# Queries in three parts with one load per lane, products over 48 and 50 rows, query sums by fours

## The chip, the cores and the metric

The kernel runs on one core of a Trainium2 chip. The metric is the device time of one execution, in microseconds; for a kernel the median of its runs stands.

## What is computed

One transformer block with conditioning: two layer norms modulated by a vector c, attention of 32 heads that share one key and value head of 16 columns, and a dense part of 512 to 1376 to 512 with gelu. All is float32, S = 2048 rows, D = 512.

```python
mod = silu(c) @ w_mod                      # sa, ca, ga, sb, cb, gb
h = layernorm(x) * (1 + ca) + sa
q = (h @ wq) as 32 heads of 16;  k = h @ wk;  v = h @ wv      # one k, one v
o = softmax(q @ k.T * 16 ** -0.5) @ v
x = x + ga * (o @ wo)
h = layernorm(x) * (1 + cb) + sb
x = x + gb * (gelu(h @ w1 + b1) @ w2 + b2)
```

## The kernel before

**Tiling.** The rows are cut into 8 blocks of 256 (HQ); each block has 8 units of 4 heads, so there are 64 units. A unit goes over the 2048 keys in 8 half-steps; the main loop (from L1424) takes two of them, X and Y, per iteration. The array of TensorE is used as two lanes of 64 rows by 128 columns: lane s = 0 uses array rows 0 to 63, lane s = 1 rows 64 to 127, each for two heads, and the lanes run side by side.

**Queries.** A projection's result is split into a high and a low part (qH, qL, float32r), which `send_q` (L436) stores in the DRAM tile dq. `load_q` (L487) brings a unit's queries back as the tile qst, one of four buffers: in each lane, rows 0 to 47 hold high, low and high part of 16 columns of q, rows 48 and 49 the high and low part of minus the row's maximum, rows 50 to 63 zeros. The key tile ks has -1 in rows 48 and 49. So one product of qst and ks gives scores less their maxima.

**Two passes.** `Max.step` (L516) makes the products m (L526) of a later unit, with rows 48 and 49 still zero; VectorE reduces each at L531. When half of a unit's maxima are done, the queries of the next unit are loaded (L534); when all are done, `put_max` (L550) turns them, splits them on POOL (L587, L141, L148) and `send` (L563) writes them by DMA into rows 48 and 49. `sexp` (L625) makes the products e (L649) from the finished qst; ScalarE takes their exponentials p (L657). The products acc (L674) multiply p with the values. A half-step has four m, four e, sixteen acc and in most of the program up to six side products, which all lie on one lane.

**Side products.** `half` (L207) issues one half of a side product on a lane. Sums of them (query projections qps, wops, w1ps, w2ps) are cut into batches, one for each iteration: lane 0 makes its half of the batch in one half-step, lane 1 its half in the next. A late query projection is `qproj_late` (L469): 12 products, so 24 halves, in batches of BATCH = 6 where (block, group) lies under LONG, else SHORT = 4. Long sums are copied out by VectorE (L477), short ones by ScalarE (L475).

**Order.** The five engines' instructions are issued in the order in which this code is run. `clock[0]` counts ticks, four per iteration; `later(n, fn)` puts work off by n ticks. At the end of an iteration (L1568) one turn of the weights' preparation is made (`state["turns"]` is 1 there): for w2 a piece is loaded, multiplied by gb on POOL (L1237) and split there (L141, L148) into w2H, w2L. There are 11 pieces. POOL also works for gelu: `inner` (L1017), a square on ScalarE (L1018) and two operations on POOL (L1019, L1020); then `tanh` on ScalarE (L1023), and the rest on POOL (L1029, L1030). The sync queue (SP) issues all DMAs.

Of the kernel before, what the change touches and what calls it, by code (L numbers as in the profile page):

```python
# [8 lines left out]
F32 = mybir.dt.float32  # L9
# [5 lines left out]
P = 128  # L15
# [21 lines left out]
MAX_WAIT = (1, 4)  # L37
QBUFS = 4
PREP = 4
BUSY = 5  # L40
BATCH = 6
SHORT = 4
LONG = (3, 1)
TAIL = (14, 9, 7)
EARLY = 5
HELD = 4
# [11 lines left out]
def raw(ap):  # L58
    return ap.bitcast(F32)
# [3 lines left out]
def adaln_mqa_mlp(  # L63
# [15 lines left out]
    nc = tc.nc  # L79
    _, S, D = x.shape  # L80
# [11 lines left out]
    HQ = BQ // 2  # L92
# [31 lines left out]
    gb = const.tile([P, D], F32, name="gb")  # L124
    b2g = const.tile([P, D], F32, name="b2g")

    dq = [[tc.dram_tile([2, 4, 16, 2, BQ], F32, name=f"dq_{b}_{g}") for g in range(KD)] for b in range(NB)]
    dz = tc.dram_tile([2, 2, HQ], F32, name="dz")
    dw1 = tc.dram_tile([NF, P, 2, KD, P], F32, name="dw1")
    drs = [tc.dram_tile([H, w], F32, name=f"drs{b}") for b, (_, w) in enumerate(blocks)]  # L130
    do = [tc.dram_tile([H // 4, 4, 32, w], F32, name=f"do{b}") for b, (_, w) in enumerate(blocks)]
# [1 line left out]
    turns = [0]  # L133
# [17 lines left out]
    clock = [0]  # L151
    state = {"mods": False, "q": NB * KD, "busy": False, "turns": 1, "lanes": (1, 0)}
# [103 lines left out]
    qbufs = [att.tile([P, 2, HQ], F32R, name=f"qst{i}") for i in range(QBUFS)]  # L256
# [1 line left out]
    qbufs = [att.tile([P, 2, HQ], F32R, name=f"qst{i}") for i in range(QBUFS)]  # L258

    def load_constants():  # L260
        nc.sync.dma_start(out=dz, in_=raw(qbufs[0][48:50]))
        with nc.allow_non_contiguous_dma(reason="1376 numbers"):
            nf_full = F // P
            nc.sync.dma_start(out=b1c[:, :nf_full], in_=b1[0:nf_full * P].rearrange("(f p) -> p f", p=P))
            if F % P:
                nc.gpsimd.memset(b1c[:, nf_full:NF], 0.0)
                nc.sync.dma_start(out=b1c[:F % P, nf_full:NF], in_=b1[nf_full * P:F].rearrange("(p f) -> p f", f=1))
# [44 lines left out]
    nc.gpsimd.memset(raw(wkL), 0.0)  # L312
    nc.gpsimd.memset(raw(ks), -1.0)
    nc.gpsimd.memset(va[:, :, 16:32], 1.0)
    for qst in qbufs:
        nc.gpsimd.memset(raw(qst), 0.0)

    def prep_wkv():
        for o, n, src in ((0, 3, 0), (48, 1, Dh), (64, 3, 0)):
# [114 lines left out]
        nc.scalar.copy(va[:, b * QT:(b + 1) * QT, 0:Dh], pv_[:, :, 16:32])  # L434

    def send_q(b, g, qH, qL):  # L436
        for t, src in enumerate((qH, qL)):
            nc.sync.dma_start(out=dq[b][g][t].rearrange("a r j n -> (a r j) n"), in_=raw(src))
        state["q"] -= 1
        sent.add((b, g))  # L440

    sent = set()
# [44 lines left out]
    def load_q(u):  # L487

        b, Q = units[u]
        r0, w = blocks[b]  # L490
        qst = qsts[u] = qbufs[u % QBUFS]
        h, g, a0 = r0 // BQ, Q // 2, (Q % 2) * 2
        cols = slice(r0 % BQ, r0 % BQ + w)
        assert (h, g) in sent
        for s in range(2):
            for r, part in ((0, 0), (16, 1), (32, 0)):
                nc.sync.dma_start(out=raw(qst[64 * s + r:64 * s + r + 16]), in_=dq[h][g][part, a0 + s][:, :, cols])
            if u >= QBUFS:
                nc.sync.dma_start(out=raw(qst[64 * s + 48:64 * s + 50]), in_=dz)

    class Max:

# [16 lines left out]
        def step(self, s, hold=None, **place):  # L519
            u, j, t, kc = self.todo[s].pop(0)  # L520
            T = blocks[units[u][0]][1] // P
            if u not in self.mx:
                self.mx[u] = att.tile([P, 4 * T, NKC], F32, name=f"mx{u}", tag="mx", bufs=2)
            m = psum.tile([P, 512], F32, name=f"m{u}_{j}_{t}_{kc}_{s}", **(place or dict(tag="m", bufs=3)))
            rows = slice(64 * s, 64 * s + 64)
            nc.tensor.matmul(m, qsts[u][rows, j, t * P:(t + 1) * P], ks[rows, kc * 512:(kc + 1) * 512],  # L526
                             start=True, stop=True)
            i = (s * 2 + j) * T + t

            def reduce():  # L530
                nc.vector.tensor_reduce(out=self.mx[u][:, i, kc:kc + 1], in_=m, axis=AX.X, op=ALU.max)  # L531
                self.left[u] -= 1
                if self.left[u] == size[u] // 2 and u > 1 and u + 1 < NU:
                    load_q(u + 1)  # L534
                if self.left[u] == 0:
                    put_max(u, self.mx.pop(u))

            self.done += 1
            if hold is None:
                reduce()  # L540
            else:
                hold(reduce)
# [7 lines left out]
    def put_max(u, mx):  # L550

        T = blocks[units[u][0]][1] // P
        qst = qsts[u]
        mm = mms[u % 2]
        turned = att.tile([P, 32], F32, name=f"turned{u}", tag="turned", bufs=2)
        if u == 0:
            pad(att, 256, "pad7")
        mt = att.tile([4 * T, P], F32, name=f"mt{u}", tag="mt", bufs=2)  # L560
        mh = att.tile([4 * T, P], F32R, name=f"mh{u}", tag="mh", bufs=2)
        ml = att.tile([4 * T, P], F32R, name=f"ml{u}", tag="ml", bufs=2)

        def send():
            for s in range(2):
                for r, src in ((48, mh), (49, ml)):
                    dst = qst[64 * s + r:64 * s + r + 1].rearrange("p j (t n) -> p (j t) n", n=P)
                    nc.sync.dma_start(out=raw(dst), in_=raw(src[2 * T * s:2 * T * (s + 1), :].unsqueeze(1)))
            placed.add(u)

        def place_first():
            for i in range(2):
                for g, piece in ((32 * i, lambda d, s: nc.scalar.copy(d, s)),
                                 (64 + 32 * i, lambda d, s: nc.gpsimd.tensor_scalar(out=d, in0=s, scalar1=1.0, scalar2=0.0, op0=ALU.mult, op1=ALU.add))):
                    piece(mt[:, g:g + 32], turned[g:g + 4 * T, :])

            def send_row(r, src):
                dst = qst[r:r + 65:64].rearrange("p j (t n) -> p (j t) n", n=P)
                nc.sync.dma_start(out=raw(dst), in_=raw(src.unsqueeze(1)))

            split(mh, ml, mt, nc.scalar, nc.gpsimd, lambda: send_row(48, mh))
            send_row(49, ml)
            placed.add(u)

        def gather():
            for g in range(0, P, 32):
                nc.gpsimd.tensor_scalar(out=mt[:, g:g + 32], in0=turned[g:g + 4 * T, :], scalar1=1.0, scalar2=0.0,  # L587
                                        op0=ALU.mult, op1=ALU.add)
            split(mh, ml, mt, nc.gpsimd, nc.gpsimd)

        def reduce():
            nc.vector.tensor_reduce(out=mm[:, :4 * T], in_=mx, axis=AX.X, op=ALU.max)
            nc.vector.transpose(out=turned, in_=mm)  # L593
            if u == 0:
                place_first()
                return
# [31 lines left out]
    def sexp(u, K, j, s, line=None):  # L628

        w = blocks[units[u][0]][1]  # L630
        qst = qsts[u]
        assert u in placed
        n = u * steps[0] + K
        if n < 3 and n not in pbufs:
            pbufs[n] = att.tile([P, 2, 2, 512], F32, name=f"p{n}", tag="p", bufs=3)
        pt = pbufs[n % 3]
        bank = banks.pop(0)
        if not bare[0]:
            banks.append(bank)
        if not isinstance(bank, int):  # L640
            e = bank
        else:
            e = psum.tile([P, 512], F32, name=f"e{u}_{K}_{j}_{s}", tag=f"e{bank}", bufs=1)
        rows = slice(64 * s, 64 * s + 64)
        if w == 512:
            kt, rhs = K, qst[rows, j, :]
        else:
            kt, rhs = 2 * K + j, qst[rows].rearrange("p j n -> p (j n)")
        nc.tensor.matmul(e, ks[rows, kt * P:(kt + 1) * P], rhs, start=True, stop=True)  # L649
        dst = pt[:, j, s, :]  # L650

        state["last"] = e

        def exp():
            if bare[0]:
                banks.append(bank)
            ins = nc.scalar.activation(dst, e, AF.Exp, scale=0.25)  # L657
            for old in written.pop((n - 3, j, s), ()):
                tc.declare_no_dep(ins.ins, old, reason="the products that read the tile's last contents come between the two")
            written.setdefault((n, j, s), []).append(ins.ins.name)  # L660
            return ins

        return exp() if line is None else line.append(exp)
# [756 lines left out]
    for u in range(NU):  # L1420
        for K in range(0, steps[u], 2):
# [145 lines left out]
                preps["w2"] = prep_w2()  # L1567
            if clock[0] >= prepared[0] + PREP and weights and weights[0] in preps and not state["busy"]:  # L1568
                prepared[0] = clock[0]
                for _ in range(state["turns"]):  # L1570
                    if weights and next(preps[weights[0]], 0) == 0:
                        weights.pop(0)
    end_step(*behind)
# [55 lines left out]
```

## Time and profile before

| | |
|---|---|
| median of 3 runs | 1549.43 us (1548.95 to 1549.63) |
| the profiled execution | 1549.17 us |
| its span, first to last instruction | 1547.4 us |
| granted TensorE clock | 1.000 over the span |
| busy: TensorE, VectorE, ScalarE, POOL | 1531.7, 1397.7, 1227.9, 666.6 us |

The profile is of one execution. Busy time is what an engine spends in instructions that compute; PE is TensorE, PEld its loading of weights, DVE VectorE, ACT ScalarE, and SPq the sync engine's queue, whose instructions issue DMAs. The chain that ended last is followed backwards from the end: each step goes to what released it, or to the instruction ahead of it on its engine. In tables of windows, an engine's busy time in a stretch stands beside the stretch's length. In timelines an "xN" is a run of like instructions, and square brackets hold the idle time ahead of an instruction with what ended it by the profile.

### The profile page before, as it was taken

What the parts mean: (1) busy time and instruction counts of PE and PEld (TensorE: products, weight loads), DVE (VectorE), ACT (ScalarE), POOL (GpSimd) and SP (SyncE); (2) the same over time, 40 slices, a digit from 0 to 9 for tenths busy, and PEclk for the clock granted to TensorE, in tenths of its full rate; (3) what the DMA queues carried; (4) which work ended last, traced back from release to release, by engine and by line L of the source; (5) the groups of instructions that cost most, each with busy time, mean ns of one, the idle gap of its engine ahead of it and who ended that gap; (6) DMA issues with size and microseconds to landing.
All of it is one profiled execution on the core that took longest, in us unless ns stands there. A gap on an engine that the chain in (4) does not pass through costs nothing.

```text
span 1547.4 us, 41604 instructions
## 1 busy us (share of the span) xinstructions
PE 1531.7 (99%) x16421; PEld 956.1 (62%) x16421; DVE 1397.7 (90%) x2493; ACT 1227.9 (79%) x2400; POOL 666.6 (43%) x1224
## 2 busy tenths in 40 slices
PE   7999999999999999999999999999999999999999
PEld 4555555567655665557655676556655676557668
DVE  7999999999999999999999999999999999999914
ACT  5677778788778887788877887788877888778874
POOL 6445524866322570246521462235711474046511
PEclk9999999999999999999999999999999999999999
DMA  8246312312030211203112120302212230213141
GB/s 261 83 132 190 133 46 91 122 59 89 16 111 19 84 60 36 94 28 101 30 51 81 55 88 23 104 26 95 62 30 74 61 100 25 84 31 99 49 151 49
DMA packets 84203, 120.85 MB, mean 78 GB/s; under 512 B 21330, under 2 KB 57426, under 8 KB 83752
## 3 DMA queue, kind: packets, MB, share of 16 engines
q1 hardware_dynamic: 84008, 118.19, 23.5%
q8 instruction: 130, 2.13, 0.6%
q14 instruction: 65, 0.53, 0.1%
HBM read 90.87 MB, written 26.74 MB: 76 GB/s over the span
## 4 chain that ended last, share of the span: by engine, by line
PE 89%; DVE 9%; DMA 1%; ACT 0%; issue 0%; POOL 0%; SPq 0%; DVEq 0%; ACTq 0%
PE acc L674 31%; PE m L526 24%; PE e L649 16%; DVE mx L531 8%; PE w1ps L207 8%; PE w2ps L207 3%; PE w2ps L196 1%; PE qps L207 1%; PE w1ps L196 1%; PE wops L207 1%; PE tp L207 1%; DVE st L859 0%; DMA wm<-in_w_mod_dram 0%; DVE x L852 0%; PE wops L196 0%; PE modr L291 0%
## 5 line engine op out<-in xcount | busy, mean ns | idle before, releaser
L531 DVE TENSOR_REDUCE mx<-m 128x1 f32<-128x512 f32 x2048 | 1269.3, 681 | 82.9 <-PE m L526 61.5
L657 ACT ACTIVATE p<-e 128x512 f32<-128x512 f32 x2048 | 1098.3, 598 | 254.7 <-PE e L649 109.3
L526 PE MATMUL m<-ks,qst 64*128 64x512 f32 x2048 | 835.2, 429 | 2.2 <-ACT bigH L394 0.8
L649 PE MATMUL e<-qst,ks 64*128 64x512 f32 x2048 | 744.3, 411 | 0.2 <-DMA qst<-ml 0.2
L674 PE MATMUL acc<-p,va 128*32 128x256 f32 x8192 | 546.9, 385 | 0.0
L526 PEld LDWEIGHTS m<-ks,qst 64*128 64x128 f32 x2048 | 366.8, 184 | 202.5 <-DVE mx L531 172.2
L649 PEld LDWEIGHTS e<-qst,ks 64*128 64x128 f32 x2048 | 364.1, 184 | 83.9 <-ACT p L657 61.7
L674 PEld LDWEIGHTS acc<-p,va 128*32 128x32 f32 x8192 | 214.9, 109 | 213.2 <-issue 109.1
L207 PE MATMUL w1ps<-h2H,w1t 64*128 64x256 f32 x1232 | 235.4, 287 | 0.0
L587 POOL TENSOR_SCALAR mt<-turned 8x32 f32<-8x32 f32 x252 | 52.3, 208 | 402.8 <-DVE turned L593 390.9
L207 PEld LDWEIGHTS w1ps<-h2H,w1t 64*128 64x128 f32 x1232 | 185.8, 184 | 28.8 <-DVE mx L531 16.0
L207 PE MATMUL w1ps<-h2L,w1t 64*128 64x256 f32 x616 | 169.2, 275 | 0.0
L207 PE MATMUL w2ps<-w2H,gH 64*128 64x512 f32 x288 | 127.2, 442 | 0.3
L207 PEld LDWEIGHTS w1ps<-h2L,w1t 64*128 64x128 f32 x616 | 114.2, 185 | 0.0
L207 PE MATMUL w2ps<-w2L,gH 64*128 64x512 f32 x288 | 112.9, 392 | 0.0
L207 PE MATMUL w2ps<-w2H,gL 64*128 64x512 f32 x288 | 112.3, 390 | 0.0
L1019 POOL TENSOR_SCALAR tt<-tt 128x256 f32<-128x256 f32 x77 | 31.0, 403 | 132.2 <-ACT tt L1018 97.3
L207 PEld LDWEIGHTS w2ps<-w2H,gH 64*128 64x128 f32 x288 | 52.9, 184 | 12.8 <-issue 2.9
L148 POOL TENSOR_TENSOR gL<-z,gH 128x256 fp32r<-128x256 f32 x77 | 56.8, 738 | 6.4
L1020 POOL TENSOR_TENSOR tt<-tt,z 128x256 f32<-128x256 f32 x77 | 56.7, 737 | 6.4
L1030 POOL TENSOR_TENSOR z<-tt,z 128x256 f32<-128x256 f32 x77 | 56.3, 731 | 6.0
L1029 POOL TENSOR_TENSOR tt<-tt,z 128x256 f32<-128x256 f32 x77 | 56.4, 732 | 0.0
(199 smaller groups left out, 1474.4 us busy)
## 6 DMA issues: line engine op xcount, KB each, us to landing
w1t<-dw SPq DMA_DIRECT2D x82, 512.0 KB
qst<-dq SPq DMA_DIRECT2D x384, 32.0 KB
do<-oc SPq DMA_DIRECT2D x62, 128.0 KB
dw<-w1s SPq DMA_DIRECT2D x11, 512.0 KB
xt<-in_A_x_dram SPq DMA_DIRECT2D x4, 1024.0 KB
dq<-qH SPq DMA_DIRECT2D x16, 256.0 KB
dq<-qL SPq DMA_DIRECT2D x16, 256.0 KB
x<-in_A_x_dram SPq DMA_DIRECT2D x8, 512.0 KB
```

The lines of the kernel that those rows point to most:

```text
L148: eng_l.tensor_tensor(out=dst_l, in0=src, in1=raw(dst_h), op=ALU.subtract)
L207: ins = nc.tensor.matmul(ps, a[rows], b_[rows], start=first_ and turn == 0, stop=last_ and turn == 1)
L526: nc.tensor.matmul(m, qsts[u][rows, j, t * P:(t + 1) * P], ks[rows, kc * 512:(kc + 1) * 512], start=True, stop=True)
L531: nc.vector.tensor_reduce(out=self.mx[u][:, i, kc:kc + 1], in_=m, axis=AX.X, op=ALU.max)
L587: nc.gpsimd.tensor_scalar(out=mt[:, g:g + 32], in0=turned[g:g + 4 * T, :], scalar1=1.0, scalar2=0.0, op0=ALU.mult, op1=ALU.add)
L649: nc.tensor.matmul(e, ks[rows, kt * P:(kt + 1) * P], rhs, start=True, stop=True)
L657: ins = nc.scalar.activation(dst, e, AF.Exp, scale=0.25)
L674: ins = nc.tensor.matmul(accs[u][32 * cidx:32 * cidx + 32, :], va[:, kt, :], rhs, start=kt == 0, stop=kt == NKT - 1)
L1019: nc.gpsimd.tensor_scalar(out=tt, in0=tt, scalar1=1.0, scalar2=1.0, op0=ALU.mult, op1=ALU.add)
L1020: nc.gpsimd.tensor_tensor(out=tt, in0=tt, in1=z, op=ALU.mult)
L1029: nc.gpsimd.tensor_tensor(out=tt, in0=tt, in1=z, op=ALU.mult)
L1030: nc.gpsimd.tensor_tensor(out=z, in0=tt, in1=z, op=ALU.add)
```

## The change

1. dq holds three parts, high, low, high, in two halves of 256 rows. `send_q` stores with three DMAs instead of two, and `load_q` loads a lane with one DMA of 48 rows instead of three of 16 (and none of zeros). The tile of zeros dz, its DMA and the four clearings of the buffers go.
2. `send` writes a row of maxima of both lanes with one DMA, so two instead of four.
3. m reads 48 rows of a lane, e 50, instead of 64.
4. LONG goes from (3, 1) to (2, 1): the four sums (2,1), (2,2), (2,3) and (3,0) go in batches of four.
5. Pieces of w2 are prepared 2, 1, 1, 2, 1, 1, ... per iteration, in place of one.

```diff
-LONG = (3, 1)
+LONG = (2, 1)
+SWIFT = (2, 1, 1)
...
-    for qst in qbufs:
-        nc.gpsimd.memset(raw(qst), 0.0)
...
     def send_q(b, g, qH, qL):
-        for t, src in enumerate((qH, qL)):
-            nc.sync.dma_start(out=dq[b][g][t].rearrange("a r j n -> (a r j) n"), in_=raw(src))
+        for part, src in ((0, qH), (2, qH), (1, qL)):
+            dst = dq[b][g][part].rearrange("h a r j n -> (a r j) h n")
+            nc.sync.dma_start(out=dst, in_=raw(src).rearrange("p (h n) -> p h n", n=HQ))
...
         for s in range(2):
-            for r, part in ((0, 0), (16, 1), (32, 0)):
-                nc.sync.dma_start(out=raw(qst[64 * s + r:64 * s + r + 16]), in_=dq[h][g][part, a0 + s][:, :, cols])
-            if u >= QBUFS:
-                nc.sync.dma_start(out=raw(qst[64 * s + 48:64 * s + 50]), in_=dz)
+            src = dq[h][g][:, r0 % BQ // HQ, a0 + s].rearrange("i r j n -> i r (j n)")
+            nc.sync.dma_start(out=raw(qst[64 * s:64 * s + 48]), in_=src)
...
-            rows = slice(64 * s, 64 * s + 64)
+            rows = slice(64 * s, 64 * s + 48)
...
         def send():
-            for s in range(2):
-                for r, src in ((48, mh), (49, ml)):
-                    dst = qst[64 * s + r:64 * s + r + 1].rearrange("p j (t n) -> p (j t) n", n=P)
-                    nc.sync.dma_start(out=raw(dst), in_=raw(src[2 * T * s:2 * T * (s + 1), :].unsqueeze(1)))
+            send_row(48, mh)
+            send_row(49, ml)
             placed.add(u)
...
-        rows = slice(64 * s, 64 * s + 64)
+        rows = slice(64 * s, 64 * s + 50)
...
-                for _ in range(state["turns"]):
+                for _ in range(SWIFT[clock[0] // 4 % len(SWIFT)] if weights == ["w2"] else state["turns"]):
```

TensorE at the start of the sum (2,1), half-steps 29 and 30 of the trace (m_1_0_... is a product m, e_6_... one e, qps_1 the sum), before:

```order
L207 MATMUL qps_1_2257<-bigH,wqH 128x512
L526 MATMUL m_1_0_0_1_2271<-ks,qst_158 128x512
L649 MATMUL e_6_0_1_2274<-qst_160,ks 128x512
L207 MATMUL qps_1_2257<-bigH,wqL 128x512
L526 MATMUL m_1_0_1_1_2278<-ks,qst_158 128x512
L207 MATMUL qps_1_2257<-bigL,wqH 128x512
L649 MATMUL e_6_1_1_2282<-qst_160,ks 128x512
L207 MATMUL qps_1_2257<-bigH,wqH 128x512
L207 MATMUL qps_1_2257<-bigH,wqL 128x512
L526 MATMUL m_1_0_2_1_2287<-ks,qst_158 128x512
L207 MATMUL qps_1_2257<-bigL,wqH 128x512
```

and after; six products of the sum in a lane's turn have become four, with m and e ahead of the first:

```order
L521 MATMUL m_1_0_0_1_2230<-ks,qst_157 128x512
L642 MATMUL e_6_0_0_2233<-qst_159,ks 128x512
L642 MATMUL e_6_0_1_2236<-qst_159,ks 128x512
L207 MATMUL qps_1_2217<-bigH,wqH 128x512
L521 MATMUL m_1_0_1_1_2240<-ks,qst_157 128x512
L207 MATMUL qps_1_2217<-bigH,wqL 128x512
L642 MATMUL e_6_1_1_2244<-qst_159,ks 128x512
L207 MATMUL qps_1_2217<-bigL,wqH 128x512
L521 MATMUL m_1_0_2_1_2248<-ks,qst_157 128x512
L207 MATMUL qps_1_2217<-bigH,wqH 128x512
L521 MATMUL m_1_0_3_1_2252<-ks,qst_157 128x512
```

TensorE again, half-step 63, the first behind the last query sum before the change:

```order
L649 MATMUL e_0_0_1_3721<-qst_157,ks 128x512
L649 MATMUL e_0_0_0_3724<-qst_157,ks 128x512
L526 MATMUL m_1_1_0_1_3727<-ks,qst_158 128x512
L526 MATMUL m_1_1_0_0_3730<-ks,qst_158 128x512
L649 MATMUL e_0_1_1_3733<-qst_157,ks 128x512
L526 MATMUL m_1_1_1_0_3736<-ks,qst_158 128x512
L526 MATMUL m_1_1_1_1_3739<-ks,qst_158 128x512
L649 MATMUL e_0_1_0_3742<-qst_157,ks 128x512
L674 MATMUL acc_3475<-p_891,va 32x256 x8
```

and the same half-step after, in which the sum (3,2) still runs:

```order
L642 MATMUL e_0_0_0_3611<-qst_156,ks 128x512
L642 MATMUL e_0_0_1_3614<-qst_156,ks 128x512
L207 MATMUL qps_2_3450<-bigL,wqH 128x512
L521 MATMUL m_1_1_1_1_3618<-ks,qst_157 128x512
L207 MATMUL qps_2_3450<-bigH,wqH 128x512
L642 MATMUL e_0_1_1_3622<-qst_156,ks 128x512
L207 MATMUL qps_2_3450<-bigH,wqL 128x512
L521 MATMUL m_1_1_2_1_3626<-ks,qst_157 128x512
L207 MATMUL qps_2_3450<-bigL,wqH 128x512
L521 MATMUL m_1_1_3_1_3630<-ks,qst_157 128x512
L642 MATMUL e_0_1_0_3633<-qst_156,ks 128x512
L667 MATMUL acc_3368<-p_875,va 32x256 x8
```

POOL around the last two pieces of w2 (w2f, w2H, w2L), tt_0_0 and tt_0_1 being the first two pieces of gelu of the first block, before:

```order
L1237 TENSOR_TENSOR w2f_4482<-w2f_4482,gb 128x512
L141 TENSOR_SCALAR w2H<-w2f_4482 128x512
L148 TENSOR_TENSOR w2L<-w2f_4482,w2H 128x512
L1237 TENSOR_TENSOR w2f_4574<-w2f_4574,gb 128x512
L141 TENSOR_SCALAR w2H<-w2f_4574 128x512
L148 TENSOR_TENSOR w2L<-w2f_4574,w2H 128x512
L1019 TENSOR_SCALAR tt_0_0_5073<-tt_0_0_5073 128x256
L1020 TENSOR_TENSOR tt_0_0_5073<-tt_0_0_5073,z_0_0_5072 128x256
L1019 TENSOR_SCALAR tt_0_1_5170<-tt_0_1_5170 128x256
L1020 TENSOR_TENSOR tt_0_1_5170<-tt_0_1_5170,z_0_1_5169 128x256
```

and after; the last two pieces of w2 now stand between the two of gelu, behind the clearing of a piece's tile that stood earlier:

```order
L1226 MEMSET w2f_4904 128x512
L1012 TENSOR_SCALAR tt_0_0_4971<-tt_0_0_4971 128x256
L1013 TENSOR_TENSOR tt_0_0_4971<-tt_0_0_4971,z_0_0_4970 128x256
L1230 TENSOR_TENSOR w2f_4819<-w2f_4819,gb 128x512
L141 TENSOR_SCALAR w2H<-w2f_4819 128x512
L148 TENSOR_TENSOR w2L<-w2f_4819,w2H 128x512
L1230 TENSOR_TENSOR w2f_4904<-w2f_4904,gb 128x512
L141 TENSOR_SCALAR w2H<-w2f_4904 128x512
L148 TENSOR_TENSOR w2L<-w2f_4904,w2H 128x512
L1012 TENSOR_SCALAR tt_0_1_5074<-tt_0_1_5074 128x256
L1013 TENSOR_TENSOR tt_0_1_5074<-tt_0_1_5074,z_0_1_5073 128x256
```

## Rows read from the trace of the kernel before

**Rows 1.** Page, chain that ended last: shares of the span by engine.
```profile
PE 89%; DVE 9%; DMA 1%; ACT 0%; issue 0%; POOL 0%; SPq 0%; DVEq 0%; ACTq 0%
```

**Rows 2.** Waits of TensorE: waited for, us in total, times, longest.
```profile
PE m L526 <- ACT bigH L394: 0.8, 1, 0.8
...
PE e L649 <- DMA qst<-ml: 0.2, 1, 0.2
```

**Rows 3.** Windows: length; busy PE, PEld, DVE, ACT, POOL (instructions); clock, DMA share, GB/s.
```profile
154.03:199.65 45.62, 45.62 (x484) 27.07 (x481) 42.25 (x73) 35.38 (x67) 25.45 (x36) 1.00 0.35 120
199.65:248.81 49.16, 49.11 (x509) 26.66 (x506) 45.59 (x78) 39.18 (x78) 8.54 (x19) 1.00 0.15 50
248.81:269.68 20.87, 20.84 (x196) 10.14 (x192) 19.93 (x36) 17.30 (x34) 11.37 (x17) 1.00 0.41 129
205.25:232.36 27.11, 27.11 (x285) 14.79 (x282) 25.03 (x43) 21.98 (x44) 3.49 (x9) 1.00 0.12 38
```

**Rows 4.** Timeline of VectorE near 233 us: start, length, instruction.
```profile
232.70 0.18 DVE L592 TENSOR_REDUCE mm<-mx 128x8 f32<-128x32 f32 x1
```

**Rows 5.** Groups of TensorE by shape: array rows*columns, operand, count, busy us, mean ns, idle.
```profile
L207 PE MATMUL qps<-bigL,wqH 64*128 64x512 f32 x96 | 37.6, 391 | 0.0
...
L173 PE MATMUL kps<-bigL,wkH 128*128 128x512 f32 x12 | 4.7, 394 | 0.0
...
L649 PEld LDWEIGHTS e<-qst,ks 64*128 64x128 f32 x2048 | 364.1, 184 | 83.9 <-ACT p L657 61.7 <-issue 2.1 <-DVE mx L531 0.5
...
L173 PEld LDWEIGHTS kps<-bigL,wkH 128*128 128x128 f32 x12 | 2.3, 188 | 0.6
```

**Rows 6.** Timeline of the sync queue at the first unit's loads.
```profile
24.04 0.34 SPq L438 DMA_DIRECT2D dq<-qL  x1
25.34 3.88 SPq L497 DMA_DIRECT2D qst<-dq  x6
```

**Rows 7.** Timeline of TensorE at the first maxima.
```profile
31.96 0.70 PE L526 MATMUL m<-ks,qst 64*128 64x512 f32 x3 [0.78 <-ACT bigH L394]
...
35.23 0.39 PE L173 MATMUL kps<-bigL,wkH 128*128 128x512 f32 x1
```

**Rows 8.** Timeline of POOL in the same stretch.
```profile
33.71 1.30 POOL L400 TENSOR_TENSOR bigL<-h,bigH 128x512 fp32r<-128x512 f32 x1
```

**Rows 9.** Timeline of the sync queue at loads of w2.
```profile
295.35 11.47 SPq L1234 DMA_DIRECT2D w2f<-in_B_w_dram  x2
```

**Rows 10.** Timeline of POOL, last two pieces of w2 and first of gelu.
```profile
328.18 1.28 POOL L1237 TENSOR_TENSOR w2f<-w2f,gb 128x512 f32<-128x512 f32 x1
...
333.59 1.30 POOL L148 TENSOR_TENSOR w2L<-w2f,w2H 128x512 fp32r<-128x512 f32 x1
335.55 0.40 POOL L1019 TENSOR_SCALAR tt<-tt 128x256 f32<-128x256 f32 x1 [0.67 <-ACT tt L1018]
...
342.02 0.74 POOL L1020 TENSOR_TENSOR tt<-tt,z 128x256 f32<-128x256 f32 x1
...
347.91 0.74 POOL L1020 TENSOR_TENSOR tt<-tt,z 128x256 f32<-128x256 f32 x1
```

**Rows 11.** Timeline of ScalarE in the same stretch.
```profile
343.88 0.42 ACT L1023 ACTIVATE tt<-tt 128x256 f32<-128x256 f32 x1
344.57 2.27 ACT L657 ACTIVATE p<-e 128x512 f32<-128x512 f32 x4 [0.27 <-PE e L649]
...
349.58 0.42 ACT L1023 ACTIVATE tt<-tt 128x256 f32<-128x256 f32 x1
```

**Rows 12.** Timeline of TensorE in a half-step with four side products.
```profile
232.94 0.39 PE L207 MATMUL qps<-bigH,wqL 64*128 64x512 f32 x1
233.16 0.39 PE L649 MATMUL e<-qst,ks 64*128 64x512 f32 x1
233.17 0.39 PE L207 MATMUL qps<-bigL,wqH 64*128 64x512 f32 x1
```

**Rows 13.** Windows again, as in rows 3, near the stores of the first queries.
```profile
20.00:24.00 4.00, 4.00 (x17) 2.95 (x17) 3.50 (x7) 2.48 (x5) 2.60 (x5) 1.00 1.09 322
```

More of the change, by code (lines that the diff above doesn't have):

```diff
@@ L125, in adaln_mqa_mlp @@
     b2g = const.tile([P, D], F32, name="b2g")
-    dq = [[tc.dram_tile([2, 4, 16, 2, BQ], F32, name=f"dq_{b}_{g}") for g in range(KD)] for b in range(NB)]
-    dz = tc.dram_tile([2, 2, HQ], F32, name="dz")
+    dq = [[tc.dram_tile([3, BQ // HQ, 4, 16, 2, HQ], F32, name=f"dq_{b}_{g}") for g in range(KD)] for b in range(NB)]
     dw1 = tc.dram_tile([NF, P, 2, KD, P], F32, name="dw1")
@@ L260, in load_constants @@
     def load_constants():
-        nc.sync.dma_start(out=dz, in_=raw(qbufs[0][48:50]))
         with nc.allow_non_contiguous_dma(reason="1376 numbers"):
@@ L492, in load_q @@
         h, g, a0 = r0 // BQ, Q // 2, (Q % 2) * 2
-        cols = slice(r0 % BQ, r0 % BQ + w)
-        assert (h, g) in sent
+        assert (h, g) in sent and w == HQ
         for s in range(2):
-            for r, part in ((0, 0), (16, 1), (32, 0)):
-                nc.sync.dma_start(out=raw(qst[64 * s + r:64 * s + r + 16]), in_=dq[h][g][part, a0 + s][:, :, cols])
-            if u >= QBUFS:
-                nc.sync.dma_start(out=raw(qst[64 * s + 48:64 * s + 50]), in_=dz)
+            src = dq[h][g][:, r0 % BQ // HQ, a0 + s].rearrange("i r j n -> i r (j n)")
+            nc.sync.dma_start(out=raw(qst[64 * s:64 * s + 48]), in_=src)
     class Max:
@@ L564, in send, with send_row @@
         def send():
-            for s in range(2):
-                for r, src in ((48, mh), (49, ml)):
-                    dst = qst[64 * s + r:64 * s + r + 1].rearrange("p j (t n) -> p (j t) n", n=P)
-                    nc.sync.dma_start(out=raw(dst), in_=raw(src[2 * T * s:2 * T * (s + 1), :].unsqueeze(1)))
+            send_row(48, mh)
+            send_row(49, ml)
             placed.add(u)
+        def send_row(r, src):
+            dst = qst[r:r + 65:64].rearrange("p j (t n) -> p (j t) n", n=P)
+            nc.sync.dma_start(out=raw(dst), in_=raw(src.unsqueeze(1)))
         def place_first():
@@ L575, in place_first @@
                     piece(mt[:, g:g + 32], turned[g:g + 4 * T, :])
-            def send_row(r, src):
-                dst = qst[r:r + 65:64].rearrange("p j (t n) -> p (j t) n", n=P)
-                nc.sync.dma_start(out=raw(dst), in_=raw(src.unsqueeze(1)))
             split(mh, ml, mt, nc.scalar, nc.gpsimd, lambda: send_row(48, mh))
```

## The prediction

> **What bounds the kernel now.** I read the page's chain first: 89% of the chain that ended last is TensorE, 9% VectorE [rows 1]. So an edit counts only where it changes what TensorE has to do, or makes it wait. The second view was TensorE's waits: past the weights of the start it waited for DMAs 0.2 us, once, for a row of maxima, and 0.8 us in the first maxima, which are put down to a ScalarE copy (I don't believe it, below) [rows 2]. Hence the small DMAs that the change takes out of the sync queue, eight a unit, stand behind no loss now. The third view was the span cut at places where the kind of half-step changes [rows 3]. (A half-step is four products m, four e, sixteen acc and whatever side products go with them; there are 64 units of 8, so 512; I number them by their groups of acc, and number 29 begins at 154.03 us.) The clock is at 2.4 GHz in all of these stretches, so it plays no part. Half-steps with six query products run at 45.62/16 = 2.851 us, those with four at 49.16/18 = 2.731, those with none at 20.87/8 = 2.609. Ten of four in a row take 27.11/10 = 2.711. The durations are one profiled execution's: 1549.17 us, of which 1.77 lie outside the span; the median of the runs is 1549.43, so 0.26 above it, and I add the sum to that median.
>
> **Query sums by fours.** The order shows that from half-step 29 on four sums, 24 side products each (12, in two lanes), are spread over six half-steps instead of four. TensorE's list is the same up to there and the same again after half-step 74; the number of products is unchanged. Before: 16 half-steps of six, 18 of four and 8 with none, 45.62 + 49.16 + 20.87 = 115.65 us for 42 half-steps. After: 42 half-steps of four, 42 x 24/6 = 168 products as before. At 2.711 that is 113.86. The 18 took 49.16 - 18 x 2.711 = 0.36 more than that: two of them are 0.18 longer, the first, where VectorE still carries the copy of the last six-product sum, and one in which it does the small reduction and the transpose of a unit's maxima [rows 4]. After the change the copy is ScalarE's (busy 39.18 of 49.16 us there, so it has room [rows 3]), but five units end in the stretch; I count three such half-steps, 3 x 0.18 = 0.54, of none to five. 113.86 + 0.54 = 114.40, so the **gain is 1.25 us**, between 0.9 (five, 114.76) and 1.8 (none). The gain exists because a half-step with none isn't 4 products shorter than one with four: 2.609 against 2.711 is 0.025 us a product, while the fifth and sixth cost 0.07 each. VectorE, busy 19.93 of 20.87 us with none, sets the short half-step; the products ride beside its maxima.
>
> **Products of 48 and 50 rows.** Their cost per row isn't in the trace at 48, but at 64 and 128: with 512 columns 391 and 394 ns, weight loads 184 and 188 ns [rows 5]. Time follows the columns; 64 rows fewer are worth 3 and 4 ns. Taken in proportion, 16 fewer rows give 0.75 ns a product and 1 ns a load; eight of each per half-step make at most 14 ns, 7 us in 512, and that if nothing lay beside anything. But loads lie under the other lane's products, and in the half-steps without side products VectorE is the limit. I take **nothing**, the row nearest to it being that the same product costs the same at twice the rows; for the range 0 to -1.5 us. Above nothing is a rival.
>
> **Start.** SP issues the two stores of q, then six loads at 3.88/6 = 0.65 us each, 25.34 to 29.22 [rows 6]. The second group of m starts at 31.96 after 0.78 us idle, put down to ScalarE's bigH [rows 7]. These products read qst and ks only, not bigH; so I take it to be the last of the loads. The change writes three parts (one more issue, 0.34 us, and half as much data again) and reads in two issues instead of six: they would be over by about 27.0 instead of 29.2, but each is three times as large and must land whole. Were the 0.78 us gone entirely, the kps products behind would move up, but the last of them, at 35.23, reads the bigL that POOL finishes at 35.01, and the m that VectorE needs next comes behind it [rows 7, 8]: at most 0.2 us is to be had. I take **-0.1**, from -0.2 to +0.5 (the later store and the larger load).
> The Trainium skill ("DMA: Bandwidth & Descriptors", section "Why a DMA increments its semaphore by 16 and not by 1") says that a transfer is spread over the largest number of engines, up to 16, that divides the slowest dimension on both sides. The new load has 48 rows on one side and 3 parts on the other, so by it 3 engines would carry 96 KB, where 16 carried each 32 KB piece. By it the start would come out at its bad end, +0.5, and the sum near 0. No row here shows engines per transfer, and the sum does not use the rule.
>
> **Loads and sends later on.** Each unit issues two loads and two sends instead of six, two of zeros, and four: eight issues fewer on SP. SP isn't waited for: TensorE's only wait for a send is the 0.2 us of unit 0 [rows 2], whose send was in two parts already. Loads are issued when half of the preceding unit's maxima are done, four half-steps or over 10.4 us ahead of their first product. In the trace SP was even held 11.47 us by a w2 load that waited for POOL, and the maxima sent behind it made nobody late [rows 2, 9]. **0**. The four memsets and the zeros lie in the start, where TensorE waits for weights anyway: 0.
>
> **Pieces of w2.** Two pieces take POOL from 328.18 to 334.89, 6.71 us, and the first of gelu (tt0) comes straight behind at 335.55, 0.40 and 0.74 with 0.1 between, to 336.78 [rows 10]. The order now starts the whole series later, at (2,1,1) per iteration, and puts the last two between tt0 and tt1. On before's axis: 336.78 + 6.67 = 343.45, then tt1's two operations, 1.23, to 344.7. ScalarE's tanh of tt1 stood at 343.88 [rows 11] and now waits about 0.85; its next exponentials stood at 344.57 after 0.27 us of waiting for TensorE, so they come 0.85 - 0.27 = 0.6 late, and TensorE behind them. tt2's product ended 348.65 - 342.76 = 5.9 after tt1's [rows 10], so now at 350.6, where its tanh stood at 349.58: 1.0 late, less the 0.6 already lost and 0.27 of slack, 0.2 more. **+0.8**, from 0 (e and p have three buffers each, which can take up some of it) to +1.1 (no slack at all). This wait stands first in ScalarE's queue, ahead of the exponentials, which is why it costs anything. Earlier POOL work is passed by the later pieces of w2, so it comes sooner than before; nothing of it is waited for.
>
> **Sum.** -1.25 + 0 - 0.1 + 0 + 0.8 = **-0.55 us**: 1549.17 - 0.55 = 1548.6 for an execution like the profiled one, 1549.43 - 0.55 = 1548.9 for the median.
>
> **Rivals.** (a) Fewer rows do shorten the products: half of the 14 ns above in each of 512 half-steps, -3.6, on top of the sum: 1545.3. For it: the 3 and 4 ns between 64 and 128 rows. Against: VectorE, busy 19.93 of 20.87 us where there are no side products [rows 3]. It decides from 5 ns a half-step.
> (b) ScalarE's buffers swallow the wait for POOL: -1.25 - 0.1 = -1.35, 1548.1. For it: ScalarE idles 0.27 us ahead of the exponentials [rows 11]. Against: it idles for TensorE, so they run in step.
> (c) **Slower**: products of 48 and 50 rows don't run beside the other lane's as those of 64 do. Now two products, one of each lane, start together (233.16 and 233.17), 0.23 us apart from those ahead (232.94), though each lasts 0.39 [rows 12]. If all pairs of m and e lost it, 4 x 0.23 x 512 = 471 us, 2020; it decides from 0.007 us a half-step, 3.7/512, under one in a hundred of that loss. For it: no product of the trace reads part of a lane. Against: the tile they are placed in stays 64 by 128, and they are issued in the same order.
> (d) The load of a lane, now one piece, lands late because fewer engines carry it. A price from rows: 16 engines, all busy, moved 322 GB/s between 20 and 24 us, 20 each [rows 13]; one alone would take 4.9 us for 96 KB, sixteen 0.3. At the start, from an issue over at 27.0 with about 1 us behind it (SP went on at 25.34 after the store issued until 24.38 [rows 6]), that is 32.9, against the 31.96 at which the second group starts now: +0.9 in place of -0.1, so 1549.9. Later 4.9 us stay inside the 10.4. Same verdict. The Trainium skill's rule above would make it three engines and a third of the 4.9.
> (e) It doesn't do what it says: if the array's time is fixed by the tile, the row counts save nothing. That is the forecast.
>
> **Chances and range.** Forecast, with (e), 0.60; (b) 0.18; (d) 0.05; (a) 0.11; (c) 0.06. What a measurement can tell from no change is about 0.2%, 3.1 us; forecast, (b) and (d) lie inside: same 0.83, faster 0.11, slower 0.06. Range: low end -1.8 - 0.2 + 0 - 1.5 = -3.5, 1545.9; high end -0.9 + 0.5 + 1.1 = +0.7, 1550.1, and 0.3 for the scatter of a median: 1550.4. What is left out, (c) and the further half of (a), is about 0.12.
>
> **What would show it.** Half-steps 29 to 70 in 113.9 to 114.8 us; idle time of ScalarE ahead of the tanh near 343 and 349 us put down to POOL's product of tt; the mean durations of m and e within 3 ns of before's, and half-steps without side products at 2.61; the second group of m between 31 and 32.5 us. The forecast is wrong if m or e or the distance between the lanes changes by more than some 5 ns, or if TensorE waits for qst anywhere past the first 70 us.

## The result and the profile after

| | before | after |
|---|---|---|
| median of 6 runs each | 1549.52 us | 1555.45 us (1554.36 to 1559.45) |
| profiled execution, its span | 1549.17, 1547.4 us | 1554.74, 1552.9 us |
| granted TensorE clock | 1.000 | 0.995 to 0.998 in the six runs |

The changed kernel is slower: the medians are 5.9 us apart, and the ratio over all runs is 1.0043 (95% interval 1.0032 to 1.0053). The forecast was 1548.9, with a range from 1545.9 to 1550.4. Line numbers have moved by 2 to 7: L521 is the product m, L642 e, L650 the exponential, L667 acc, L494 the query load, L436 the store.

The page of the changed kernel, first lines and two groups of its costliest:

```profile
span 1552.9 us, 40943 instructions
...
PE 1535.2 (99%) x16421; PEld 956.4 (62%) x16421; DVE 1394.6 (90%) x2489; ACT 1228.6 (79%) x2404; POOL 664.3 (43%) x1220
...
L521 PE MATMUL m<-ks,qst 48*128 48x512 f32 x2048 | 840.7, 432 | 3.4 <-ACT xt L366 1.3
L642 PE MATMUL e<-qst,ks 50*128 50x512 f32 x2048 | 749.0, 414 | 0.4 <-DMA qst<-ml 0.2
```

TensorE is as busy as before in share, so the page alone doesn't tell where 5.5 us of span went. I set the starts of the half-steps of both traces side by side (505 groups of acc can be told apart). The changed kernel is late by 4.6 us at half-step 5, by 2.5 at 55, by 3.6 at 75, by 4.2 at 110, and from there to the end it loses 0.8 more, little by little. So there is one large loss in the first 90 us, then the gain of the query sums, and some small losses. (These starts are of one execution each.)

**The start.** Timeline of SP in the changed kernel (compare [rows 6]):

```profile
24.75 0.46 SPq L436 DMA_DIRECT2D dq<-qL  x1
27.36 1.64 SPq L494 DMA_DIRECT2D qst<-dq  x2
```

and of TensorE (compare [rows 7]):

```profile
32.03 0.47 PE L521 MATMUL m<-ks,qst 48*128 48x512 f32 x1 [0.76 <-DMA qst<-dq]
33.76 0.70 PE L521 MATMUL m<-ks,qst 48*128 48x512 f32 x3 [1.25 <-ACT xt L366]
```

The loads begin at 27.36 instead of 25.34, are issued by 29.0, and the second group of m starts at 33.76 instead of 31.96. That is 1.8 us late, and it stays 1.8 up to the first e at 70.68 (68.88 before). This time the profile names the load for the first of the two waits. For the second it names a ScalarE operation on xt that m doesn't read, as it named one on bigH before; but in the trace the second load's semaphore gets its last update at 33.62 (31.77 for the last of the six loads before), just ahead of the product, so that wait is for the load too.

Not all of the 1.8 us is the loads'. TensorE's first query product, which stands ahead of the stores and the loads, is late already. Its line before, and after:

```profile
17.50 0.40 PE L173 MATMUL qps<-h0H,wqH 128*128 128x512 f32 x1
```
```profile
18.22 0.39 PE L173 MATMUL qps<-h0H,wqH 128*128 128x512 f32 x1
```

That is 0.7 us, and it lies inside the scatter between executions: in kernels 2, 3 and 5 below, whose start is that of the kernel before, this product begins at 17.31, 18.83 and 17.40. The share of the stores and loads is the other 1.1 us.

**The clock.** Windows of the changed kernel, columns as in [rows 3]:

```profile
69.80:73.80 4.00, 3.68 (x19) 1.62 (x15) 4.00 (x8) 3.20 (x7) 2.01 (x4) 1.00 0.13 34
73.80:81.66 7.86, 7.69 (x50) 3.73 (x49) 6.08 (x12) 3.80 (x7) 0.07 (x1) 0.57 0.02 8
81.66:90.00 8.34, 8.34 (x94) 5.00 (x90) 7.08 (x12) 6.12 (x12) 1.62 (x7) 1.00 0.20 57
```

Inside the second window, from 74.2 to 81.05 us by the trace, the granted clock is at its lower level, 1.2 GHz: 6.8 us, which makes the window's mean 0.57. By half-step 5 the 1.8 us have become 4.6, so this stretch cost 2.8.

**The query sums**, half-steps 29 to 70 of the changed kernel: 114.63 us against 115.65 [rows 3].

```profile
158.69:273.32 114.63, 114.53 (x1180) 62.03 (x1176) 106.21 (x181) 91.83 (x181) 35.56 (x59) 1.00 0.31 102
```

**ScalarE's wait for POOL**, timeline of ScalarE (compare [rows 11]):

```profile
348.30 0.42 ACT L1016 ACTIVATE tt<-tt 128x256 f32<-128x256 f32 x1 [0.67 <-POOL tt L1013]
348.63 2.26 ACT L650 ACTIVATE p<-e 128x512 f32<-128x512 f32 x4
...
354.18 0.42 ACT L1016 ACTIVATE tt<-tt 128x256 f32<-128x256 f32 x1 [0.45 <-POOL tt L1013]
```

Both tanh wait for POOL, and the exponentials follow at once, where before they waited 0.27 us for TensorE. The two half-steps there took 3.25 and 3.02 us instead of 2.84 and 2.85: 0.58 together.

### The profile page after: what moved, and what is told of

Its sections match the earlier page's. It is cut to its first block, busy times and chain, and to the rows that moved or that the text cites. A ratio compares the mean times of both kernels' runs of the same rounds, so it can differ in the third digit from the quotient of the medians.

```text
span 1552.9 us, 40943 instructions
## 1 busy us (share of the span) xinstructions
PE 1535.2 (99%) x16421; PEld 956.4 (62%) x16421; DVE 1394.6 (90%) x2489; ACT 1228.6 (79%) x2404; POOL 664.3 (43%) x1220
## 4 chain that ended last, share of the span: by engine, by line
PE 87%; DVE 9%; POOL 2%; ACT 1%; issue 0%; DMA 0%; SPq 0%; DVEq 0%; POOLq 0%; ACTq 0%
PE acc L667 30%; PE m L521 21%; PE e L642 14%; DVE mx L526 8%; PE w1ps L207 8%; PE w2ps L207 6%; PE qps L207 3%; PE w2ps L196 1%; PE wops L207 1%; PE w1ps L196 1%; PE tp L207 1%; DVE st L852 0%; DVE x L845 0%; PE wops L196 0%; PE modr L290 0%
## 5 line engine op out<-in xcount | busy, mean ns | idle before, releaser
L650 ACT ACTIVATE p<-e 128x512 f32<-128x512 f32 x2048 | 1097.2, 598 | 255.3 <-PE e L642 131.6
L521 PE MATMUL m<-ks,qst 48*128 48x512 f32 x2048 | 840.7, 432 | 3.4 <-ACT xt L366 1.3
L642 PE MATMUL e<-qst,ks 50*128 50x512 f32 x2048 | 749.0, 414 | 0.4 <-DMA qst<-ml 0.2
L667 PE MATMUL acc<-p,va 128*32 128x256 f32 x8192 | 548.0, 386 | 0.0
L521 PEld LDWEIGHTS m<-ks,qst 48*128 48x128 f32 x2048 | 371.9, 186 | 209.6 <-DVE mx L526 181.0
L642 PEld LDWEIGHTS e<-qst,ks 50*128 50x128 f32 x2048 | 367.4, 186 | 69.5 <-ACT p L650 53.0
L667 PEld LDWEIGHTS acc<-p,va 128*32 128x32 f32 x8192 | 215.2, 109 | 213.6 <-issue 109.8
```

The lines of the kernel that those rows point to most:

```text
L667: ins = nc.tensor.matmul(accs[u][32 * cidx:32 * cidx + 32, :], va[:, kt, :], rhs, start=kt == 0, stop=kt == NKT - 1)
```

## The experiments

First the parts one by one, on the kernel before (later runs than the result's, each with runs of the kernel before beside them, whose medians were 1549.5 to 1550.0).

**1. Loads and stores alone.**

```diff
...
-            for r, part in ((0, 0), (16, 1), (32, 0)):
-                nc.sync.dma_start(out=raw(qst[64 * s + r:64 * s + r + 16]), in_=dq[h][g][part, a0 + s][:, :, cols])
+            src = dq[h][g][:, r0 % BQ // HQ, a0 + s].rearrange("i r j n -> i r (j n)")
+            nc.sync.dma_start(out=raw(qst[64 * s:64 * s + 48]), in_=src)
```

The stores are made in three parts, and dq is laid out for them. (In code, "..." marks what is left out.)

> The kernel before with the stores in three parts and one load of 48 rows per lane alone; rows read, sends, zeros, query sums and pace of w2 stay as before. Theory (the whole loss is the start: the first loads land late, and the granted TensorE clock falls once near 74 us): second group of m at 33.5 to 34 us instead of 31.96, everything behind it 1.8 us later, and a stretch of some 5 to 10 us at 1.2 GHz behind 70 us that costs 2 to 6 us more; in all 1553 to 1558 us. Rival (the clock falls because products read 48 and 50 rows, or the loss lies in the half-steps): +1.8 us at most, 1551.3, clock 1.000.

1554.24 us, ratio 1.0026 (1.0014 to 1.0037): the theory had the size right, but not where the clock falls. TensorE's waits and windows of this trace:

```profile
PE m L526 <- DMA qst<-dq: 3.0, 2, 1.7
```
```profile
32.00:34.00 2.00, 0.46 (x1) 0.18 (x1) 1.94 (x4) 2.00 (x4) 1.75 (x3) 0.85 0.88 227
34.00:36.00 2.00, 1.26 (x4) 0.65 (x4) 0.47 (x1) 1.13 (x2) 1.98 (x3) 0.50 1.03 369
36.00:38.00 2.00, 2.00 (x5) 1.61 (x6) 1.42 (x3) 0.00 (x0) 1.71 (x3) 0.50 1.00 331
```

Here the waits for the load are plain, 3.0 us in two, and the clock falls in the second of them, at 33.4 us, not near 74. By half-step 5 this kernel is 5.3 us late (0.7 of it already at the first query product) and loses nothing more. The four runs with a clock of 0.996 to 0.998 took 1553.6 to 1556.5, the two at 1.000 took 1550.4 and 1551.7. So the loads and stores by themselves make the loss, in two pieces: a late start, and in most runs a fall of the clock.

**2. Four query sums by fours alone.** `LONG = (2, 1)`.

> The kernel before with four query sums in batches of four instead of six, alone. Theory: half-steps 29 to 70 take 114.5 us instead of 115.65, no half-step elsewhere changes, clock 1.000: -1.1 us, 1548.4. Rival (the gain read from the changed kernel came with the fewer DMAs and semaphores): 0 to -0.4.

1556.05 us, 1.0039 (1.0026 to 1.0051): both theories missed. Half-steps 29 to 70 took 114.60, as forecast, but three half-steps near 340 us lost 7.2 us. SP's and TensorE's timelines of this kernel:

```profile
315.94 14.73 SPq L1234 DMA_DIRECT2D w2f<-in_B_w_dram  x2
330.76 0.66 SPq L568 DMA_DIRECT2D qst<-mh  x1
```
```profile
335.45 0.46 PE L649 MATMUL e<-qst,ks 64*128 64x512 f32 x1 [0.96 <-DMA qst<-ml]
...
342.92 0.79 PE L649 MATMUL e<-qst,ks 64*128 64x512 f32 x1 [3.08 <-ACT p L657]
```

The sums end later, so the pieces of w2 begin later: a load of w2 waits 14.7 us on SP for a buffer that POOL still uses, the maxima queue behind it and land late, and the first tanh waits for POOL 3.3 us. In the 3.1 us wait the clock falls, and it is at 1.2 GHz from 342 to 349 us.

**3. Pieces of w2 at 2, 1, 1 alone.** `SWIFT = (2, 1, 1)` at L1570.

> The kernel before with the pieces of w2 made 2, 1, 1 per iteration, alone. Theory: ScalarE's tanh of the second and third piece of gelu waits for POOL, two half-steps near 344 and 350 us grow by 0.6 together and one to three later ones by some 0.2 each: +0.6 to +1.1 us, 1550.1 to 1550.6, clock 1.000. Rival (the waits in the changed kernel come from the query sums, which end later there): 0.

1556.40 us, 1.0042 (1.0029 to 1.0055): missed too. ScalarE's tanh waits for nothing here. But more loads of w2 stand on SP ahead of the units' loads and maxima, TensorE waits 1.6 us for a tile's zeros and 3.0 us for maxima, and the clock falls in the second of these waits, at 297 us:

```profile
PE e L650 <- DMA qst<-ml: 3.2, 2, 3.0
PE m L527 <- DMA qst<-dz: 1.6, 1, 1.6
```

**4. 48 and 50 rows alone.**

> The kernel before with m reading 48 and e 50 rows of a lane, alone. Theory: nothing, 1549.5 within 0.4 us, mean durations of m and e within 1 ns of 429 and 411, clock 1.000. Rival (part of a lane is slower, or is what brings the clock down): 1551 or more, clock under 1.

1550.91 us, 1.0008 (0.9999 to 1.0017): between theory and rival. No wait, no stretch at 1.2 GHz in the trace, whose execution had a clock of 1.000; but five of the eleven runs had 0.998 or 0.999. More of this below.

**5. The sums and the pieces of w2 together**, on the kernel before.

> The kernel before with the query sums by fours and the pieces of w2 at 2, 1, 1 together; loads, sends and rows as before. Theory (each of the two alone pushed pieces of w2 into the way of the maxima's transfers, together they fit, as in the changed kernel): no wait of TensorE for qst past 70 us, clock 1.000, 1549 to 1550 us. Rival (they fit only because the change takes DMAs off the sync queue): waits of 1 us or more for qst between 270 and 350 us, clock under 1, 1553 or more.

1550.46 us, 1.0006 (0.9997 to 1.0014). No wait for qst past 70 us, as in the changed kernel: the two parts that cost 6 us each alone cost nothing clear of the scatter together. The trace has half-steps 29 to 70 in 114.63, the two longer half-steps with the tanh (0.62 together) and three later ones 0.1 to 0.35 longer each. It also has a short fall of the clock, from 72.6 to 76.1 us, though its start isn't late; it cost 1.2 us:

```profile
72.00:74.00 2.00, 1.89 (x11) 0.70 (x15) 2.00 (x4) 1.39 (x3) 0.00 (x0) 0.66 0.06 17
74.00:76.00 2.00, 2.00 (x16) 1.03 (x10) 0.97 (x3) 0.00 (x0) 0.00 (x0) 0.50 0.00 0
```

**6. The changed kernel with the start repaired.** The first sum is stored in two parts, the first two units loaded in pieces, the third part stored behind them.

```diff
...
+            for i in range(3 if u < 2 else 0):
+                nc.sync.dma_start(out=raw(qst[64 * s + 16 * i:64 * s + 16 * i + 16]), in_=src[i % 2])
...
```

> The changed kernel, but the first query sum is stored in two parts and the first two units are loaded in pieces of 16 rows, as before; its third part is stored behind those loads. Theory (the first store and the first loads cost the start 1.8 us, and that late start is what brings the clock down near 74 us): second group of m at 31.5 to 32.3 us, clock 1.000, nothing late at half-step 5; the rest as in the changed kernel, -1.1 for the query sums and +0.9 for ScalarE's waits for POOL: 1549 to 1550 us. Rival (the fall of the clock near 74 us has another cause, in the sends or the rows): start repaired, clock 0.998 again, 1552 to 1554.

1550.23 us, 1.0005 (0.9996 to 1.0014); clock 1.000 in nine of eleven runs. By half-step 5 it is 0.2 us late instead of 4.6. The loss of the changed kernel is nearly all in the stores and loads of the first units.

**7. Store or load?** The store in three parts stays, only the first two units are loaded in pieces.

```diff
...
+            for i in range(3 if u < 2 else 0):
+                nc.sync.dma_start(out=raw(qst[64 * s + 16 * i:64 * s + 16 * i + 16]), in_=src[i])
...
```

> The changed kernel, with the first query sum still stored in three parts, but the first two units loaded in pieces of 16 rows (six issues a unit) instead of one load of 48 rows per lane. It tells the store from the load. Theory (the load of 48 rows takes 2 us longer to land, the three-part store lands 1.2 us later, the four issues saved give 2.3 us back): loads issued from 27.3 to some 30.5 us, second group of m at 33 to 33.8, so the start stays 1.3 to 1.8 us late, clock under 1 in most runs: 1551 to 1555 us. Rival (the load's form alone costs the start): second group of m at 32 us, 1550, clock 1.000.

1551.15 us, 1.0008 (0.9999 to 1.0017). My theory fell. The rival holds for the start, not for the clock: five of the eleven runs had 0.998 or 0.999. SP and TensorE:

```profile
25.62 3.55 SPq L495 DMA_DIRECT2D qst<-dq  x6
```
```profile
31.59 0.70 PE L524 MATMUL m<-ks,qst 48*128 48x512 f32 x3 [0.17 <-PE m L524]
```

The same three-part store, and the first load goes out at 25.62 instead of 27.36: a piece of 16 rows reads one part and goes when that has landed, the load of 48 rows reads all three and goes when the last of them has, at 27.23 by the trace. And six issues that end at 29.2 are there for a product at 31.59, two that end at 29.0 for one at 33.76. So the form of the load costs twice: it starts 1.7 us later, which eats what the four issues less would save, and it lands later behind its issue (the last landing is at 33.62, here at 31.39).

**8. What is left without the sums and the pace** (kernel 6 with the sums by sixes and one piece per iteration).

> The changed kernel with the start as in the first of these kernels, and with the query sums in batches of six and the pieces of w2 one per iteration as before the change: what is left is the single loads, the sends in two and the rows of 48 and 50. Theory (these are worth nothing past the start): 1549.5 within 0.7 us, clock 1.000. Rival (fewer DMAs give something): 1548.5 or less; rival (rows cost something): 1550.5 or more.

1551.26 us, 1.0014 (1.0005 to 1.0023): the rival with a cost. Its profiled execution, at a clock of 1.000, is 0.5 us late by half-step 5 and loses another 0.7 to the end; seven of eleven runs lie under 1.000 (0.997 to 0.999). The single loads past the start and the sends in two show no gain. (Its first query product, too, is 0.8 us later than in the trace of before, so the 0.5 is scatter; five of the seven runs had 0.997 or 0.998.)

**9. A version that should beat both**: three sums by fours, `LONG = (2, 2)`, and SWIFT; on the kernel before, and on kernel 6.

> The kernel before with three query sums by fours instead of four (LONG = (2, 2)) and pieces of w2 at 2, 1, 1; loads, sends and rows as before. The pieces of w2 begin an iteration earlier than with four sums, and the last two stand before the first piece of gelu again. Theory (ScalarE's wait for POOL comes from the two pieces between the first and second piece of gelu): no longer half-steps near 344 and 350 us, half-steps 29 to 70 some 0.85 us shorter than before, no wait for qst past 70 us, clock 1.000: 1548.8 us. Rival (the pieces made earlier push the normalisation on POOL back, TensorE waits there near 315 us): 1550.5 or more.

> The same two changes on the changed kernel with its start repaired: rows of 48 and 50, one load per lane past the first two units, sends in two. Against the other kernel of this call it tells what rows and DMAs are worth together. Theory (rows of 48 and 50 cost 1 us over the program, DMAs nothing): stretch from half-step 110 to 500 longer by 0.6 to 1.2 us than in the other, 1549.8 us. Rival (nothing): the two within 0.3 us of each other.

1552.52 us, 1.0016 (1.0007 to 1.0025), and 1550.64, 1.0005 (0.9996 to 1.0013). In both the last two pieces of w2 stand before gelu and the tanh wait for nothing: the theory of that wait holds. But on the kernel before, TensorE waits for maxima again, near 315 us (0.46 and 0.83), where the rival had it:

```profile
314.48 0.46 PE L650 MATMUL e<-qst,ks 64*128 64x512 f32 x1 [0.46 <-DMA qst<-ml]
315.78 0.46 PE L650 MATMUL e<-qst,ks 64*128 64x512 f32 x1 [0.83 <-DMA qst<-ml]
```

The second kernel, with 8 DMAs fewer a unit, has no such wait. So the fewer DMAs, worth nothing by themselves, most likely make room for another pace; the two kernels differ in rows as well. From half-step 110 to 500 the second took 0.5 us longer than the first, a little less than its theory had. Neither beats the kernel before, and no version here does.

**10. The clock.** Four kernels asked what lets it fall near 74 us. Fillers are products whose result nobody reads. The edit of the first kernel, in the list that gives the order of the start, where w16 stands for sixteen fillers and m1 for a step of the first maxima:

```diff
-x3.1:p x3.0:p w16 m1 x3.2:a lm2 m1 m1 ...
+x3.1:p x3.0:p w19 m1 w6 x3.2:a lm2 m1 m1 ...
```

> The changed kernel with nine more filler products on TensorE, three ahead of the first m and six between the first and the second, where it waits for the loads. Theory (waiting in the start lets the clock fall): start late by 1.8 to 2.2 us as before, but clock 1.000 and no slow stretch near 74 us: 1551 to 1552.5 us. Rival (the slow stretch hangs on what is done near 70 us, not on the start): clock 0.998 again, 1554 to 1557.

> The changed kernel with twelve filler products on TensorE, two behind six of the m in half-steps 0 and 1, the thin stretch from 70.7 to 75 us that VectorE's maxima set and at whose end the clock falls. The start stays late. Theory (the clock falls because of that thin stretch, where TensorE has 18 products in 4.5 us): clock 0.999 or 1.000 in most runs, no stretch at 1.2 GHz near 74 us, only the 1.8 us of the start lost: 1551 to 1552.5. Rival (it is the wait of the start, or neither): clock 0.995 to 0.998 as in the changed kernel, 1554 to 1556.

> The kernel before with eight more filler products on TensorE ahead of the first m: everything behind comes some 1.9 us later, and TensorE doesn't wait longer for a load. It tells whether the clock falls because TensorE waits in the start, or because what comes near 70 us is shifted against something else. Theory (waiting): clock 1.000, 1551.4 us. Rival (shift): clock under 0.9985 in half of the runs or more, with a stretch at 1.2 GHz near 74 us, 1553 to 1556.

> The kernel before with two loads of modulation weights moved on the sync queue ahead of the first unit's query loads: the loads stay in pieces of 16 rows, but start some 1.7 us later and TensorE waits for them. Theory (any late first load costs what the changed kernel lost): second group of m at 33.4 to 34 us, 1.5 to 2 us lost by half-step 5, clock under 0.9985 in half of the runs or more: 1552 to 1556. Rival (the fall of the clock needs the changed kernel's other parts): 1551.3, clock 1.000.

| kernel | us, ratio (95%) | runs with a clock of 0.998 or less |
|---|---|---|
| changed kernel | 1555.45, 1.0043 | 6 of 6 |
| fillers in the start | 1555.03, 1.0034 (1.0022 to 1.0047) | 3 of 5 |
| fillers near 72 us | 1558.53, 1.0051 (1.0038 to 1.0063) | 3 of 5 |
| loads and stores alone (1) | 1554.24, 1.0026 | 4 of 6 |
| before, start late by fillers | 1550.45, 1.0007 (0.9998 to 1.0016) | 0 of 11 |
| before, weight loads first | 1549.70, 1.0001 (0.9992 to 1.0010) | 0 of 11 |

With fillers in the start the wait for loads shrank to 0.4 us and the start was 2.1 us late; two runs kept the clock (1552.7 and 1552.9), three didn't (1555.0 to 1556.4). With fillers near 72 us it was the same, two (1555.9, 1556.0; the fillers and a start 2.3 us late cost this) against three (1558.5 to 1559.6). So where the clock falls it costs about 3 us, and filling the wait or the thin stretch doesn't keep it from falling. Only executions at 1.000 were profiled of these two, so where it fell in the other runs isn't known. The third kernel came out only 0.7 us late: its first m is 1.9 us later than before, its fifth 0.6. So it tells less than meant. The fourth failed as a test: with 1 MB of weights ahead of them on the queue the first piece landed at 30.29 us instead of 27.55, but the last at 31.79 instead of 31.77 (second group of m at 31.93), and the kernel ran as before. What stands is a count: with the first unit in one load per lane 16 of 22 runs had a clock of 0.998 or less; with it in pieces 12 of 99 (all kernels of this section but 2 and 3, which have waits of their own), and the kernel before 2 of 100. The 12 have something in common: all are of kernels that read 48 and 50 rows (4, 6, 7, 8 and the second of 9), 12 of their 55 runs, against none of 44 where 64 rows are read. So the load isn't all that brings the clock down. Whether the rows do, or the later loads and sends that come with them in all of these but 4, isn't shown; 4 has 2 of its 11.

## Why the prediction failed, point by point

**Start: the step that failed.** The term stood at -0.1, from -0.2 to +0.5; in the profiled execution the start is 1.8 us late, 1.1 of it behind the first query product, where the change acts. (Two traces of section 10 have the same loads, one of them with fillers beside them; counted the same way, their starts lose 2.1 and 1.9.) I had counted what the fewer issues save on SP, and the later store and the larger load at +0.5 at worst. Rival (d) named the right mechanism, a load that is late since it comes in one piece, at +0.9, and gave it a chance of 0.05. Two errors made it small. The load of 48 rows waits for all three stores, and SP went on at 27.36, where I had put the loads 0.34 us behind those of [rows 6], at 25.7; and I took kps and bigL as a cover [rows 7, 8] that hides the end of the chain. That cover bounds what an earlier load can give, not what a later one costs. From the end of the issue to the product it takes 4.8 us, against 2.7 before. By the rule of the Trainium skill ("DMA: Bandwidth & Descriptors", section "Why a DMA increments its semaphore by 16 and not by 1") the new load is carried by 3 engines instead of 16, which speaks for a slower landing. The trace agrees: the semaphore of the first load of 48 rows gets one update at 28.62, right behind its issue, and three more from 30.89 to 31.90; that of the first 16-row piece in the kernel before gets sixteen, from 27.36 to 27.55.

**The clock: a term that the sum did not have.** I wrote that it plays no part, since it was 1.000 in the stretches read. It was, in the kernel before. The 6.8 us at 1.2 GHz cost the profiled execution 2.8. With 1.8 that makes the 4.6 by half-step 5; the runs lie between 1554.4 and 1559.5, most likely because such stretches are longer or more than one in some of them (their clocks, 0.998 to 0.995, speak for it; only one was profiled).

**Query sums: right.** 114.63 us for half-steps 29 to 70, forecast 114.40: a gain of 1.02 for 1.25. Two half-steps took 2.90 for 2.71 and three 2.78, where I had counted three of 2.89.

**Pieces of w2: right in place, a little less in size.** The two waits stand where they were put, 0.41 and 0.17 us, forecast 0.6 and 0.2. Rival (b), that the buffers swallow them, is out. But I costed the rest of this part at nothing with the words that nothing of POOL's work was waited for. That holds only because the sums and the pace were changed together, as 2, 3 and 5 show.

**Rows: right that they give nothing; they cost.** Half-steps 260 to 400 (140 of them, no waits) took, by trace:

```
64 rows: 394.30 before, 393.98 (1), 394.01 (2), 394.04 (3), 394.24 (5), 394.35 and 394.28 (10), 394.27 (9)
48, 50:  394.42 after, 394.46 (4), 394.68 (6), 394.36 (7), 394.47 (8), 394.40 and 394.41 (10), 394.41 (9)
```

Each of the eight with fewer rows is above each of the eight with 64, if only by 0.01 where they come closest; the means differ by 0.27 us, 1.9 ns a half-step, some 1 us in 512 as an estimate. It is a rough one: among kernels run beside each other the gap goes from 0.01 (the start made late in 10, and 7) to 0.45 (1 to 3, and 4). In the groups from 400 to 1400 us of kernel 1 and of kernel 4 m went from 428 to 429 and e from 408 to 410 ns (428 and 409 before, 429 and 411 after):

```profile
L526 PE MATMUL m<-ks,qst 64*128 64x512 f32 x1421 | 589.6, 428 | 0.6
L649 PE MATMUL e<-qst,ks 64*128 64x512 f32 x1421 | 520.5, 408 | 0.0
```
```profile
L526 PE MATMUL m<-ks,qst 48*128 48x512 f32 x1421 | 589.9, 429 | 0.6
L649 PE MATMUL e<-qst,ks 50*128 50x512 f32 x1420 | 518.5, 410 | 0.0
```

So rival (a) is out, and rival (c) has the right sign with about a quarter of the 7 ns from which it would have decided. Why fewer rows take longer isn't settled, nor whether they are what brings the clock down more often (10).

**Loads and sends later on: right.** Past 71 us the changed kernel's TensorE waits for no DMA.

**The sum as measured:** +0.7 (ahead of the first query product) + 1.1 (first loads) + 2.8 (clock) - 1.0 (sums) + 0.6 (tanh) + 0.5 (three half-steps near 565 and 642 us, cause open) + 0.3 (the rest up to the last half-step, the rows in it) + 0.5 (behind the last half-step) = +5.5, the difference of the two spans.

## What to carry to other kernels

Merging small DMAs into one helps only where somebody waits for the queue; in a start where TensorE waits for the landing, ask of the merged one what it must wait for and how long it takes to land behind its issue, and keep the small form there. A kernel whose order was set around POOL and one DMA queue can't be priced part by part: two parts that cost 6 us each cost nothing clear of the scatter together. One trace against one trace carries the scatter of both, here 0.7 us at the start: look how late a stretch is already where the edit begins to act. And a clock of 1.000 in the trace of before is no promise for a change that makes TensorE late or idle: give it a term, here some 3 us.

## What was not expected of the hardware

In the five traces that show it the fall of the clock came at 33, 73, 74, 297 and 342 us. Three of these times, at 33, 297 and 342, TensorE stood in a wait of 1.7 to 3.1 us; each fall cost 1 to 4 us, about as much as such a wait itself. In the changed kernel it came 40 us behind its wait, with TensorE shown busy for 3.68 of the 4.00 us up to 73.8, and with fillers at either place the clock still fell in three runs of five, so what triggers it there stays open. A layout of dq in which the 48 rows of a lane follow one another, so that the single load might spread wider, was not tried.
